# Head 0 built by engines, three hash passes instead of four, and a later landing time in the list schedule

## Chip, cores and metric

The kernel runs on one core of one Trainium2 chip. The metric is device time in microseconds (us) of one execution; the median of several runs is compared. Engines go by the profile's names: PE (matrix multiplication, with PEld for its weight loads), DVE (vector), ACT (activation), POOL (GpSimd) and SP, which here only issues DMA transfers.

## What is computed

Attention whose mask comes from a hash of q and k, followed by two dense blocks. The reference, cut to what matters:

```python
# q, k, v: (2, 8, 768, 64), proj: (64, 6); 16 heads in all
q_bits = (einsum('bhsd,dk->bhsk', q, proj) > 0); k_bits = the same of k
mask   = q_bucket[:, :, :, None] == k_bucket[:, :, None, :]     # all six bits equal
scores = where(mask, scale * q @ k.T, -1e9)
attn   = softmax(scores) @ v                                    # (+1e-9 below the sum)
x = attn as (1536, 512)
x = ((x @ w1) * (x @ w2)) @ w3 @ w_out                          # d_ff 1024
out = (sigmoid(x @ w_gate) * (x @ w_val)) @ w_out2              # d_ff 1536
```

The weights arrive as 64-bit floats and are decoded to 32 bits on the chip.

## The kernel before

**Stages.** The 16 heads are worked through one after the other, each in six score tiles g of 128 rows by 768 columns (96 in all). Beside them runs filler: the product of w3 and w_out (`gen_fill`), then the first dense block for the first 512 tokens (`gen_first`). After that `moe` does all the rest. Nearly all matrix products are split into a high and a low part of each operand and made of three passes.

**One head** (`prep`). q and k are transposed on PE and copied by ACT into `aq` and `ak`: rows 0 to 63 hold the high parts, rows 64 to 127 the low parts. A head's scores need four 128-row operands, `aq`, `bq`, `ak` and `bk`, put together by DMAs on SP's queue: `bq[0:64]` from `aq` (line 393), `bk[0:64]` from `ak`'s low rows (395), the hash rows `ft` into `bk[64:128]` and `bq[64:128]` (406, 407), and `ak[64:128]` from `ak`'s high rows (408). The hash rows come of a PSUM tile `gps` for each half of 384 columns: `aq` by the high and by the low part of the projection, then `ak` by both, four passes (401); DVE compares with zero (402). Head 0 has its own code, `first_head`: there the copies of `bq[0:64]` (433) and of `ak[64:128]` (436) are DMAs, and the rest is done by ACT and DVE. `prep` of the next head is spread over the current head's steps: the passes of `gps` come two steps after the transposes of q.

**One score tile.** Four matmuls (466, 469), a row maximum on DVE (476, 477), the exponential on ACT (487), transposes into two PSUM tiles `tp` (520), the split of those by ACT and DVE (523, 524), and for two tiles together twelve matmuls with v (537). `emit_x` brings the upper 64 rows of that result through ACT into a tile `xu` (546) and adds the lower ones on DVE (548).

**Shared things.** `tp`, `gps`, the transposes of q and k, the sums with v and the filler's accumulators (`w3t`, `wacc`, `p0`, `y0`) all come from one ring of four PSUM buffers, `psT` (line 285), which is handed out in program order. Weight tiles of 512 KB are loaded ahead by `stage_next` (318) and decoded by `decode` on ACT, POOL and DVE (334 to 343). Score tiles have two buffers, `scs`.

**Order.** Everything up to `moe` is put in order by a list schedule that runs while the kernel is built (`order_engines`): each engine takes the ready instruction with the lowest priority number, by costs written into the code. A transfer on SP's queue lands, by that model, 1080 ns after its issue plus bytes/360 ns plus 900 ns (lines 217 and 218). The resulting order is fixed for each engine; at run time an instruction that isn't ready holds up what is queued behind it on its engine. `Tiles.holds` adds one rule by hand: the fourth weight load may not be issued before the transfer named `late["c0"]`, which is line 433.

Of the kernel before, what the change touches and what calls it, by code (L numbers as in the profile page):

```python
# [44 lines left out]
def order_engines(tc):  # L45
# [122 lines left out]
    while events:  # L168
        now = events[0][0]
        while events and events[0][0] <= now:  # L170
            _, _, what, x = heapq.heappop(events)
            if what == "ready":
                heapq.heappush(ready[eng[x]], (ins[x].bass_priority, x))
            elif what == "slot":
                g = rings[x][0]
                slots[g] += 1
                pools[g[0]] -= 1
                wake(g)
                if not pools[g[0]]:
                    wake(g[0])  # L180
            elif what == "end":
                for u in ends[x]:
                    left[u] -= 1
                    at[u] = max(at[u], now + step.get((eng[x], eng[u]), 60))
                    if not left[u]:
                        post(at[u], "ready", u)
                for t in held.get(x, ()):
                    todo[t] -= 1
                    if not todo[t]:
                        post(now + 200, "slot", t)  # L190
        again = True
        while again:
            again = False
            for e in ranks:
                while free[e] <= now and ready[e]:
                    _, k = heapq.heappop(ready[e])
                    g = blocked(k)
                    if g is not None:
                        waiting.setdefault(g, []).append(k)
                        continue  # L200
                    for t in opens.get(k, ()):
                        g = rings[t][0]
                        slots[g] -= 1
                        taken[g] += 1
                        if slots[g] > 0 and waiting.get(g):
                            wake(g)
                            again = True
                    order[e].append(k)
                    for u in begins[k]:
                        left[u] -= 1  # L210
                        at[u] = max(at[u], now)
                        if not left[u]:
                            post(at[u], "ready", u)
                    free[e] = done = now + cost(k)
                    if e == "SP":
                        n = count(ins[k].outs[0]) * list(ins[k].outs[0].ap)[0][1] * mybir.dt.size(ins[k].outs[0].dtype)
                        dma = max(now + 1080, dma) + n / 360
                        done = dma + 900
                    post(done, "end", k)
                    post(free[e], "free", k)  # L220
    assert sum(map(len, order.values())) == N, "the list schedule is stuck"
# [7 lines left out]
def lsh_attention_moe_moe2_kernel(  # L229
# [48 lines left out]
    def f(ap):  # L278
        return ap.bitcast(F32)
# [8 lines left out]
    idr = cst.tile([P, P], F32R, name="idr")  # L288
    pq_raw = cst.tile([P, NB], F32, name="pq_raw")
    pq = [[cst.tile([P, P], F32R, name=f"pq{a}{i}") for i in range(2)] for a in "qk"]  # L290
    thr = cst.tile([P, 2], F32, name="thr")
    lim = cst.tile([P, 2], F32, name="lim")

# [16 lines left out]
    def stage_next():  # L310

        if units:
            dst, src = units.pop(0)
            alt[0] += 1
            other = late.get("mp") or (wp if "mw" not in late else dec)
            t = (other if alt[0] % 2 else dec).tile([P, CH], U64, tag="st", name="st", bufs=2)
            shp = dst.shape
            ld = sync.dma_start(out=t if len(shp) == 2 else t.rearrange("p (k f) -> p k f", k=shp[1]), in_=src)
            if "c0" in late and alt[0] == 4:
                Tiles.holds.append((ld.ins.name, late["c0"].name))  # L320
            staged.append((dst, t))

# [27 lines left out]
    def load_head(h, nms):  # L350
        if not 0 <= h < NH:
            return
        b, hh = divmod(h, H)
        for nm, src in (("q", q), ("k", k), ("v", v)):
            if nm in nms:
                t = ap_.tile([P, NT, D], F32, tag="raw" + nm, name=f"raw{nm}{h}", bufs=1)
                sync.dma_start(out=t, in_=src[b, hh].rearrange("(p c) d -> p c d", c=NT))
                raws[h, nm] = t

    def split(h, nm, part):  # L360
# [17 lines left out]
    def prep(h):  # L378

        load_head(h, "v")  # L380
        if h < NH:
            alloc_mats(h)
            m = mats[h]
            for nm, d in (("q", "aq"), ("k", "ak")):
                t = splits[h, nm]
                for half in range(2):
                    ps = psT.tile([P, 512], F32R, tag="t", name="trr")
                    for c in range(3):
                        pe.transpose(ps[:, c * P:(c + 1) * P], t[:, half * 3 + c].rearrange("p a d -> p (a d)"), idr)
                    act.activation(out=m[d][:, half * HS:(half + 1) * HS], in_=f(ps[:, :HS]), func=AF.Copy,  # L390
                                   scale=SCALE if nm == "q" else 1.0)
                    if nm == "q" and half == 1:
                        sync.dma_start(out=f(m["bq"][0:D]), in_=f(m["aq"][0:D]))
                    yield
            sync.dma_start(out=f(m["bk"][0:D]), in_=f(m["ak"][D:P]))
            for half in range(2):
                hs = slice(half * HS, (half + 1) * HS)
                ps = psT.tile([P, 512], F32, tag="t", name="gps")
                for n, nm in enumerate(("aq", "ak")):
                    for x in range(2):  # L400
                        pe.matmul(ps[:, :HS], lhsT=pq[n][x], rhs=m[nm][:, hs], start=n + x == 0, stop=n + x == 2)  # L401
                dve.tensor_scalar(out=m["ft"][:, hs], in0=ps[:, :HS], scalar1=thr[:, 0:1], scalar2=thr[:, 1:2],
                                  op0=ALU.is_gt, op1=ALU.mult)
                if half == 0:
                    yield
            sync.dma_start(out=f(m["bk"][D:P]), in_=f(m["ft"][0:D]))
            sync.dma_start(out=f(m["bq"][D:P]), in_=f(m["ft"][D:P]))
            sync.dma_start(out=f(m["ak"][D:P]), in_=f(m["ak"][0:D]))
            yield
        for nm in "qk":  # L410
            split(h + 1, nm, 0)
            split(h + 1, nm, 1)
        load_head(h + 2, "qk")
        split(h - 1, "v", 0)
        split(h - 1, "v", 1)

    def first_head():
# [6 lines left out]
        for nm, d in (("q", m["aq"]), ("k", kt)):  # L424
            t = splits[0, nm]
            for half in range(2):
                ps = psT.tile([P, 512], F32R, tag="t", name="trr")
                for c in range(3):
                    pe.transpose(ps[:, c * P:(c + 1) * P], t[:, half * 3 + c].rearrange("p a d -> p (a d)"), idr)
                kps = (kps + [ps])[-2:]  # L430
                act.activation(out=d[:, half * HS:(half + 1) * HS], in_=f(ps[:, :HS]), func=AF.Copy, scale=SCALE if nm == "q" else 1.0)
            if nm == "q":
                late["c0"] = sync.dma_start(out=f(m["bq"][0:D]), in_=f(m["aq"][0:D])).ins
        for half in range(2):
            act.activation(out=m["ak"][0:D, half * HS:(half + 1) * HS], in_=f(kps[half][0:D, :HS]), func=AF.Copy)
        sync.dma_start(out=f(m["ak"][D:P]), in_=f(kt[0:D]))
        for half in range(2):
            act.activation(out=m["bk"][0:D, half * HS:(half + 1) * HS], in_=f(kps[half][D:P, :HS]), func=AF.Copy)
        load_head(1, "qk")
# [100 lines left out]
    def emit_x(u):  # L540
        acc = av_t.pop(u)
        h, t = divmod(2 * u, NT)
        b, hh = divmod(h, H)
        r0 = (hh % 2) * D
        xu = ap_.tile([P, 2 * P], F32, tag="xu", name=f"xu{u}", bufs=1)
        act_copy(xu[r0:r0 + D], acc[D:P, :2 * P])
        x = xall[r0:r0 + D, hh // 2, b * S + t * P:b * S + (t + 2) * P]
        dve.tensor_tensor(out=x, in0=acc[0:D, :2 * P], in1=xu[r0:r0 + D], op=ALU.add)
        if t == NT - 2 and h % 2 == 1:
            emit_scale(h)  # L550

# [255 lines left out]
    for n, (r0, sg) in enumerate(((D, 1.0), (0, -1.0))):  # L807
        for x in range(2):
            dve.memset(f(pq[n][x]), 0.0)
        for b0, sgn in ((r0, sg), (r0 + o, -sg)):  # L810
            hi, lo = (t[:, b0:b0 + NB] for t in pq[n])
            dve.tensor_scalar(out=hi, in0=pq_raw, scalar1=sgn, scalar2=None, op0=ALU.mult)
            dve.scalar_tensor_tensor(out=lo, in0=pq_raw, scalar=sgn, in1=f(hi), op0=ALU.mult, op1=ALU.subtract)
    dve.memset(thr[D:P, 1:2], -BIG)
    dve.memset(thr[0:D, 1:2], 1.0)
    dve.memset(thr[:, 0:1], 0.0)
# [108 lines left out]
```

## Time and profile before

| | us |
|---|---|
| median of 3 runs | 849.06 (848.66 to 849.44) |
| profiled execution, its own time | 851.55 |
| span of that execution, first to last instruction | 849.0 |
| PE busy | 806.6 (95%) |
| DVE busy | 567.4 (67%) |
| ACT busy | 523.9 (62%) |
| mean granted clock of TensorE | 0.983 |

PE is busy for 95% of the span, but that is a mean over stages in which different engines are nearly full. The table of stretches shows each by itself. The granted clock is a share of full speed: 1.0 is 2.4 GHz, 0.5 is 1.2 GHz.

### The profile page before, as it was taken

How to read it: one execution, taken by the hardware profiler on the slowest of the kernel's cores; microseconds unless marked ns; L12 is line 12 of the kernel's file. 1: busy time of each engine (PE TensorE's matmuls, PEld its weight loads, DVE VectorE, ACT ScalarE, POOL GpSimd, SP SyncE). 2: the span in 40 equal slices, each digit the busy share in tenths (PEclk: the TensorE clock that was granted, in tenths of full speed). 3: DMA queues.
4: the chain of work that ended last, by engine and by line, in shares of the span. 5: the costliest groups of instructions: out<-in, count | busy, mean ns of one | idle time of the engine just before them, and what ended most of it. 6: DMA issues, size and time to landing. Idle time of an engine off the chain costs nothing.

```text
span 849.0 us, 12225 instructions
## 1 busy us (share of the span) xinstructions
PE 806.6 (95%) x4272; PEld 685.3 (81%) x4272; DVE 567.4 (67%) x967; ACT 523.9 (62%) x1024; POOL 336.6 (40%) x328
## 2 busy tenths in 40 slices
PE   4788999999989999999999989999999999999998
PEld 4677898989878989888788768778888888888886
DVE  5998988897889988997489999972222222222222
ACT  4887887877878998787356665653334333343331
POOL 2564334342345453338544546543332333323330
PEclk7898999999999999999999999999999999999999
DMA  7655554344335644221115443300001000010001
GB/s 225 176 177 169 160 133 130 88 108 109 85 106 134 159 126 104 83 91 54 50 49 160 153 134 122 127 0 1 1 0 38 14 1 0 1 50 1 0 1 49
DMA packets 44908, 71.54 MB, mean 84 GB/s; under 512 B 6128, under 2 KB 32752, under 8 KB 44848
## 3 DMA queue, kind: packets, MB, share of 16 engines
q1 hardware_dynamic: 44848, 70.78, 29.2%
q8 instruction: 33, 0.54, 0.3%
q14 instruction: 27, 0.22, 0.1%
HBM read 52.43 MB, written 3.19 MB: 66 GB/s over the span
## 4 chain that ended last, share of the span: by engine, by line
PE 69%; DVE 18%; issue 6%; ACT 4%; DMA 3%; SPq 0%; DVEq 0%; ACTq 0%
PE pa L698 12%; PE pb L698 12%; PE m L698 11%; PE av L537 6%; PE tp L520 6%; PE p L698 5%; PE wacc L593 4%; PE s L466 3%; DVE da L337 3%; PE s L469 3%; DVE da L338 3%; PE gps L401 2%; PE y L698 2%; DVE pt L524 2%; DVE s L476 1%
## 5 line engine op out<-in xcount | busy, mean ns | idle before, releaser
L738 DVE TENSOR_TENSOR pb<-pb,a 128x512 f32<-128x512 f32 x52 | 36.2, 695 | 138.8 <-PE pb L698 134.8
L336 POOL TENSOR_SCALAR da<-da 128x512 f32<-128x512 f32 x76 | 54.1, 712 | 137.3 <-ACT da L334 136.3
L524 DVE TENSOR_TENSOR pt<-tp,pt 128x384 fp32r<-128x384 f32 x192 | 101.1, 549 | 6.5 <-ACT pt L523 4.9
L520 PE MATMUL tp<-idf,e 128*128 128x128 f32 x576 | 101.2, 278 | 3.1 <-ACT ak L390 1.4
L487 ACT ACTIVATE e<-s,sm 128x768 f32<-128x768 f32 x96 | 95.8, 999 | 13.0 <-DVE sm L477 12.8
L692 POOL TENSOR_TENSOR wal<-xall,wah 128x512 fp32r<-128x512 f32 x36 | 46.9, 1302 | 137.9 <-ACT wah L276 137.9
L523 ACT ACTIVATE pt<-tp 128x384 fp32r<-128x384 f32 x192 | 90.3, 494 | 17.9 <-PE tp L520 16.1
L476 DVE TENSOR_REDUCE s<-s 128x1 f32<-128x768 f32 x96 | 91.9, 957 | 13.0 <-PE s L469 12.8
L698 PE MATMUL pa<-x,wah 128*128 128x512 f32 x320 | 98.9, 389 | 0.0
L698 PE MATMUL pb<-x,wbh 128*128 128x512 f32 x320 | 98.5, 389 | 0.0
L520 PEld LDWEIGHTS tp<-idf,e 128*128 128x128 f32 x576 | 72.7, 143 | 14.7 <-ACT ak L390 2.3
L537 PE MATMUL av<-pt,spv 128*128 128x256 f32 x576 | 79.5, 289 | 0.2 <-DVE pt L524 0.2
L334 ACT ACTIVATE da<-st 128x512 f32<-128x512 f32 x76 | 51.0, 671 | 43.9 <-DVE w1r L343 17.9
L537 PEld LDWEIGHTS av<-pt,spv 128*128 128x128 f32 x576 | 73.5, 194 | 2.6 <-DVE pt L524 0.6
L466 PE MATMUL s<-ak,aq 128*128 128x384 f32 x192 | 63.7, 389 | 10.4 <-ACT e L487 8.9
L593 PE MATMUL wacc<-wo,t 128*128 128x512 f32 x192 | 70.5, 427 | 0.5 <-ACT wo L276 0.2
L698 PEld LDWEIGHTS pb<-x,wbh 128*128 128x128 f32 x320 | 60.1, 188 | 12.4
L698 PEld LDWEIGHTS pa<-x,wah 128*128 128x128 f32 x320 | 60.1, 188 | 12.4
L338 DVE SCALAR_TENSOR_TENSOR da<-st,da 128x512 uint32<-128x512 uint32 x76 | 65.9, 867 | 1.3
L698 PE MATMUL pb<-x,wbl 128*128 128x512 f32 x160 | 62.2, 389 | 0.0
L698 PE MATMUL pa<-x,wal 128*128 128x512 f32 x160 | 62.2, 389 | 0.0
L469 PE MATMUL s<-bk,bq 128*128 128x384 f32 x192 | 59.0, 367 | 0.0
(159 smaller groups left out, 1899.1 us busy)
## 6 DMA issues: line engine op xcount, KB each, us to landing
st<-in_moe_w_dram SPq DMA_DIRECT2D x32, 512.0 KB, 3.9
st<-in_moe_w_out_dram SPq DMA_DIRECT2D x20, 512.0 KB, 3.5
st<-in_moe_w_gate_dram SPq DMA_DIRECT2D x12, 512.0 KB, 3.5
st<-in_moe_w_val_dram SPq DMA_DIRECT2D x12, 512.0 KB, 3.6
rawq<-in_q_dram SPq DMA_DIRECT2D x16, 192.0 KB, 3.1
rawk<-in_k_dram SPq DMA_DIRECT2D x16, 192.0 KB, 3.7
rawv<-in_v_dram SPq DMA_DIRECT2D x16, 192.0 KB, 2.4
bq<-aq SPq DMA_DIRECT2D x16, 192.0 KB, 2.6
```

The costliest lines, as they stand in the source:

```text
L336: pool.tensor_scalar(out=f(a), in0=f(a), scalar1=F64_HI, scalar2=F64_LO, op0=ALU.min, op1=ALU.max)
L338: dve.scalar_tensor_tensor(out=a, in0=hw, scalar=0xC0000000, in1=a, op0=ALU.bitwise_and, op1=ALU.bitwise_or)
L466: pe.matmul(s[:, half, :HS], lhsT=m["aq"][:, qs], rhs=m["ak"][:, ks], start=True, stop=False)
L469: pe.matmul(s[:, half, :HS], lhsT=m["bq"][:, qs], rhs=m["bk"][:, ks], start=False, stop=True)
L476: dve.tensor_reduce(out=one[:, 1:2], in_=s[:, :, :HS], op=ALU.max, axis=AX.XY, negate=True)
L487: act.activation(out=e.rearrange("p (a c) -> p a c", a=2), in_=s[:, :, :HS], func=AF.Exp, bias=sm[:, 1:2], scale=sm[:, 0:1], accum_out=su_ ...
L520: pe.transpose(ps[:, j * P:(j + 1) * P], e[:, c * P:(c + 1) * P], idf)
L523: act.activation(out=dh, in_=src, func=AF.Copy)
L524: dve.tensor_tensor(out=lo[:, g % 2, half * 3:half * 3 + 3], in0=src, in1=f(dh), op=ALU.subtract)
L537: pe.matmul(acc[:, :2 * P].rearrange("p (a t) -> p a t", a=2), lhsT=w, rhs=r[:, :, c], start=(c == 0 and i == 0), stop=(c == NT - 1 and i ...
L593: pe.matmul(acc, lhsT=t3[x][:, j], rhs=wo[y][:, j], start=(j == 0 and n == 0), stop=(j == NF1 - 1 and n == 2))
L698: mm = pe.matmul(ps, lhsT=lhs[x], rhs=rhs[y], start=start and n == 0, stop=stop and n == 2)
```

## The change

Five edits:

- Head 0: `bq[0:64]` is copied by POOL instead of a DMA. `ak[64:128]` is copied by DVE straight from the PSUM tiles of the transposed k, instead of a DMA from SBUF.
- Head 0's loads: the third weight load, not the fourth, is held, until head 1's load of k is issued.
- Heads 1 to 15: the hash rows take three passes instead of four. The third pass multiplies `bq`, whose lower rows hold the high rows of q and whose upper rows get a copy of the high rows of k by one more DMA, with a new constant `pl` that holds both low parts of the projection. The product of the low part of the projection with the low parts of q and k is no longer formed. The upper rows of `bq` are overwritten with hash rows later, as before.
- `emit_x`: ACT writes the upper rows straight into `xall`, and DVE adds in place; the tile `xu` is gone.
- The list schedule takes a transfer to land 2400 ns instead of 900 ns after its last byte.

```diff
-                        done = dma + 900
+                        done = dma + 2400
...
+    pl = cst.tile([P, P], F32R, name="pl")
...
-            if "c0" in late and alt[0] == 4:
+            if "c0" in late and alt[0] == 3:
...
-                sync.dma_start(out=t, in_=src[b, hh].rearrange("(p c) d -> p c d", c=NT))
+                ld = sync.dma_start(out=t, in_=src[b, hh].rearrange("(p c) d -> p c d", c=NT))
+                if h == 1:
+                    late["c0"] = ld.ins
...
+            sync.dma_start(out=f(m["bq"][D:P]), in_=f(m["ak"][0:D]))
             sync.dma_start(out=f(m["bk"][0:D]), in_=f(m["ak"][D:P]))
...
-                for n, nm in enumerate(("aq", "ak")):
-                    for x in range(2):
-                        pe.matmul(ps[:, :HS], lhsT=pq[n][x], rhs=m[nm][:, hs], start=n + x == 0, stop=n + x == 2)
+                for n, nm in enumerate(("aq", "ak", "bq")):
+                    pe.matmul(ps[:, :HS], lhsT=pq[n][0] if n < 2 else pl, rhs=m[nm][:, hs], start=n == 0, stop=n == 2)
...
-                late["c0"] = sync.dma_start(out=f(m["bq"][0:D]), in_=f(m["aq"][0:D])).ins
+                pool.tensor_copy(m["bq"][0:D], f(m["aq"][0:D]))
...
-            act.activation(out=m["ak"][0:D, half * HS:(half + 1) * HS], in_=f(kps[half][0:D, :HS]), func=AF.Copy)
-        sync.dma_start(out=f(m["ak"][D:P]), in_=f(kt[0:D]))
+            hs = slice(half * HS, (half + 1) * HS)
+            act.activation(out=m["ak"][0:D, hs], in_=f(kps[half][0:D, :HS]), func=AF.Copy)
+            dve.tensor_copy(m["ak"][D:P, hs], f(kps[half][0:D, :HS]))
...
-        xu = ap_.tile([P, 2 * P], F32, tag="xu", name=f"xu{u}", bufs=1)
-        act_copy(xu[r0:r0 + D], acc[D:P, :2 * P])
         x = xall[r0:r0 + D, hh // 2, b * S + t * P:b * S + (t + 2) * P]
-        dve.tensor_tensor(out=x, in0=acc[0:D, :2 * P], in1=xu[r0:r0 + D], op=ALU.add)
+        act_copy(x, acc[D:P, :2 * P])
+        dve.tensor_tensor(out=x, in0=acc[0:D, :2 * P], in1=x, op=ALU.add)
...
+    for n in range(2):
+        (act_copy if n else dve.tensor_copy)(pl[n * D:(n + 1) * D], f(pq[n][1][n * D:(n + 1) * D]))
```

## Rows read from the trace of the kernel before

**Rows 1.** Busy time by stretch, all engines; clock 1.00 is full speed.

```profile
core 0: us, PE busy (x) PEld busy (x) DVE busy (x) ACT busy (x) POOL busy (x), PEclk, DMA share, GB/s
0.00:20.00 20.00, 8.26 (x36) 7.50 (x36) 11.23 (x40) 9.08 (x17) 3.81 (x11) 0.80 0.81 237
20.00:83.00 63.00, 52.32 (x305) 44.26 (x304) 59.01 (x109) 52.34 (x107) 32.87 (x36) 0.88 0.59 170
83.00:100.00 17.00, 15.92 (x108) 14.17 (x106) 16.14 (x30) 13.20 (x28) 8.87 (x10) 0.99 0.50 141
100.00:220.00 120.00, 118.06 (x798) 106.47 (x797) 104.21 (x202) 94.30 (x200) 36.78 (x46) 1.00 0.45 117
220.00:240.00 20.00, 15.58 (x112) 14.00 (x111) 16.93 (x34) 17.12 (x37) 11.63 (x12) 1.00 0.46 117
240.00:383.00 143.00, 140.39 (x936) 126.70 (x935) 129.48 (x256) 121.79 (x259) 61.14 (x67) 0.99 0.42 112
383.00:435.00 52.00, 51.50 (x229) 42.18 (x228) 33.79 (x37) 28.58 (x52) 33.41 (x23) 1.00 0.13 41
435.00:565.00 130.00, 124.22 (x531) 98.22 (x530) 123.81 (x160) 82.84 (x149) 65.38 (x61) 1.00 0.39 122
565.00:849.00 284.00, 280.30 (x1237) 231.85 (x1235) 72.81 (x105) 104.69 (x177) 82.72 (x64) 1.00 0.03 12
```

**Rows 2.** Timeline 0 to 20: start, duration, engine, line, instruction, idle before it.

```profile
5.94 1.00 POOL L369 TENSOR_TENSOR spv<-rawv,spv 128x384 fp32r<-128x384 f32 x1 [4.64 <-DVE spv L366]
8.05 0.62 SPq L436 DMA_DIRECT2D ak<-ft  x1
8.56 1.25 DVE L450 TENSOR_SCALAR bk<-gps,thr 64x384 fp32r<-64x384 f32 x2 [2.70 <-PE gps L447]
9.83 1.29 DVE L450 TENSOR_SCALAR bq<-gps,thr 64x384 fp32r<-64x384 f32 x2
13.08 0.62 DVE L366 CAST spq<-rawq 128x384 fp32r<-128x384 f32 x1 [1.96 <-DMA rawq<-in_q_dram]
16.25 0.36 DVE L366 CAST spk<-rawk 128x384 fp32r<-128x384 f32 x1 [0.80 <-DMA rawk<-in_k_dram]
17.11 1.01 PE L466 MATMUL s<-ak,aq 128*128 128x384 f32 x2 [1.48 <-DMA ak<-ft]
17.91 0.84 PE L469 MATMUL s<-bk,bq 128*128 128x384 f32 x2
18.80 0.97 DVE L476 TENSOR_REDUCE s<-s 128x1 f32<-128x768 f32 x1 [1.12 <-PE s L469]
```

**Rows 3.** Chain that ended last, in order of time: start, duration, what.

```profile
8.05 9.02 DMA ak<-ft
254.45 1.39 PE gps L401 x8
```

**Rows 4.** Timeline around head 15's hash rows, 338 to 345.

```profile
338.19 0.82 PE L520 MATMUL tp<-idf,e 128*128 128x128 f32 x6
338.19 0.46 SPq L395 DMA_DIRECT2D bk<-ak  x1
339.55 0.51 PE L401 MATMUL gps<-aq,pqq 128*128 128x384 f32 x2
340.44 0.68 DVE L402 TENSOR_SCALAR ft<-gps,thr 128x384 fp32r<-128x384 f32 x1
341.42 0.51 PE L401 MATMUL gps<-aq,pqq 128*128 128x384 f32 x2
342.83 0.67 DVE L402 TENSOR_SCALAR ft<-gps,thr 128x384 fp32r<-128x384 f32 x1
```

**Rows 5.** DMA issues by tile: count, KB each, median us from issue to landing.

```profile
bk<-ak SPq DMA_DIRECT2D x15, 192.0 KB, 2.7
bq<-ft SPq DMA_DIRECT2D x15, 192.0 KB, 4.1
```

**Rows 6.** Timeline, head 11: its last transfer issued, its first score matmuls.

```profile
257.43 0.61 SPq L407 DMA_DIRECT2D bq<-ft  x1
268.01 0.52 PE L466 MATMUL s<-ak,aq 128*128 128x384 f32 x2
```

**Rows 7.** What PE waited for, 0 to 385: us, times, longest.

```profile
PE s L466 <- ACT e L487: 8.9, 7, 4.1
PE trr L389 <- DVE pt L524: 2.6, 5, 1.0
PE tp L520 <- DVE xall L548: 1.2, 3, 0.6
```

**Rows 8.** Groups of instructions, whole span: busy us, mean ns, idle before.

```profile
L366 POOL CAST spk<-rawk 128x384 fp32r<-128x384 f32 x14 | 7.9, 568 | 15.1 <-PE trr L389 14.8 <-DMA rawk<-in_k_dram 0.3
L276 ACT ACTIVATE xu<-av 64x256 f32<-64x256 f32 x48 | 18.3, 380 | 15.5 <-PE av L537 14.3
L548 DVE TENSOR_TENSOR xall<-av,xu 64x256 f32<-64x256 f32 x48 | 19.9, 415 | 13.5 <-ACT xu L276 12.8
```

**Rows 9.** Busy time in a stretch of half clock, columns as in rows 1.

```profile
76.00:84.00 8.00, 6.83 (x29) 6.33 (x30) 5.81 (x12) 4.59 (x9) 1.21 (x3) 0.57 0.49 177
```

## Prediction

> **What bounds the kernel now.** I read the busy time by stretch first, because the mean of 95% PE hides which engine is full where. In [rows 1] the first 20 us are bound by nothing that is busy: PE works 8.26 us of them, DVE 11.23. From 20 to 83 DVE works 59.01 of 63 us (94%) and PE 83%, so DVE sets the pace there. From 83 to 383 PE works 290.0 of 300 us (15.92, 118.06, 15.58 and 140.39) and DVE 88%: PE is the bound, and the only gap worth the name is the 4.4 us in 220 to 240. After 383 the change touches no instruction; PE is the bound from 383 to 435 and from 565 to the end, DVE from 435 to 565. A shift of the first 383 us should therefore be passed on whole.
>
> Then I read the timeline of the first 20 us [rows 2]. The hash rows of head 0 are done at 9.83 + 1.29 = 11.12, but the first scores start at 17.11, and the row names what they wait for: the DMA that copies `ak`. The chain [rows 3] gives its price, 9.02 us from issue to landing. Its own row and the DMA column of [rows 1] say why: at 0.81 share and 237 GB/s it stands behind the first weight loads.
>
> **Head 0.** With POOL and DVE copies, what comes last for the first score tile is the first half of the hash rows of q: `bq` is written by two instructions from 9.83 on, the first done near 10.5. `ak`'s DVE copies lie in the gap of 2.70 us before 8.56 [rows 2]. They aren't in the trace; the nearest rows are the two compares of 64x384 out of PSUM, 1.25 us, and half of that would be a gain on nothing, so I take 1.25 and it fits the gap. POOL's copy of 768 columns is at most twice a cast of 384 columns, 2 x 0.568 = 1.14 us [rows 8]; put before POOL's 1.00 us at 5.94 it ends near 7.1, behind it near 8.1, in both cases before 10.5. So the covers hold by over 1 us; gone, they would cost the same amount at most.
>
> The first row maximum can then start at about 10.5 + 0.2 + 0.84 (the second pair of score matmuls at the pace of [rows 2]) = 11.6 to 11.8, in place of 18.80: 7.0 us sooner. Not all of that is a gain, since DVE is what is full from 20 us on. The gain is DVE's idle time that gets filled. In [rows 2] the gaps are 1.96 (wait for the load of head 1's q), 0.80 (load of its k) and 1.12 (first scores). The last two vanish: there is softmax work to do, and the new hold lets the load of k pass a weight load of 512 KB, some 2 us at 237 GB/s. Of 1.96 I take away 1.0, as the first maximum (0.97) fits into it. 1.0 + 0.80 + 1.12 = **2.9 us**. Bounds: 0, if DVE's decode work was going to fill later gaps anyway, and 7.0, if everything moves with the first scores.
>
> The Trainium skill, on the page "SBUF — State Buffer", section "Who interferes with whom", holds that a POOL instruction and a DVE copy or cast in its two-port mode block each other for a whole instruction. By that rule the cast at 4.08 to 5.86 could lose up to one POOL copy, and the first scores would come up to 1.1 us later, a time near 845.6, inside the range of the forecast. No row here shows that pair; the copies read PSUM.
>
> **Three passes.** Eight passes of a head take 1.39 us in a run without a break [rows 3], 0.174 each. Two of eight fall away: 0.35 us a head. Heads 4 to 15 have them in the stretch that PE bounds, 12 x 0.35 = **4.2 us**. Heads 1 to 3 have them while DVE is full, so I count nothing there (5.2 if they count).
>
> **The price of the third pass.** It needs a copy of `ak`'s high rows in `bq`, by a DMA that can't be issued before `ak` is complete. In [rows 4] the sister copy is issued at 338.19, just as `ak` is done; the first pass runs at 339.55, 1.4 us later, and the compare ends at 341.12. A copy of this kind lands 2.7 us after issue [rows 5], and the new list schedule allows it 1080 + 546 + 2400 ns = 4.0 us, so it will put the third pass at about 342.2 and the compare near 343.3: each half keeps its PSUM buffer up to 2.2 us longer than the 1.6 us of today (the second half is less, 0.6 here). Both halves together take two of the four `psT` buffers, a filler accumulator mostly the third, so the transposes have one for a while. What is queued behind on PE isn't stuck, as the schedule knows of the wait and fills it with scores, sums with v and filler, as far as buffers allow. PE waits little [rows 7] for readers of that ring today (2.6 and 1.2 us). The buffers lost are 3 to 6 buffer-us a head, that is 0.7 to 1.5 us if all four were always in demand. Lower end nothing, upper end 1.0 us a head or 12 us. I take 0.2 us a head, **2.5 us** over 12 heads, nearer to the low end since DVE and ACT have a tenth of their time free there [rows 1] and can catch up.
>
> The DMAs behind it (lines 406 to 408) go out later by 1 to 3 us. They are due when the next head's scores begin: head 11 has the last one issued at 257.43 and its first scores at 268.01 [rows 6], and 4.1 us of landing [rows 5] leave 6.5 us. So that costs nothing; with the cover gone, at most what exceeds it. The added DMA waits on SP for what its neighbour, line 395, waits for already, so nothing new is stuck behind it; its issue is 0.46 us [rows 4].
>
> **In place, and the order.** ACT's 380 ns and DVE's 415 ns stay as they are, and ACT waited for PE there, not for the single buffer of `xu` [rows 8]: nothing. The constant `pl` costs two small copies at 5 us, in idle time. The later landing time shifts every consumer of a transfer in the order. At run time hardly any engine waits for a transfer after 20 us; it can mend little, and can move decode work behind where it was wanted, above all in the gap of 220 to 240. PE's idle time between 83 and 383 is 10.0 us [rows 1]; a new order may win or lose some 4 of it, about the size of that gap. I take 0.
>
> **Sum.** The profiled execution's span is 849.0 us, its own time 851.55; the median of the runs is 849.06, 2.49 below that, and I subtract from the median. 849.06 - 2.9 - 4.2 + 2.5 = **844.5 us**.
>
> **Rivals.**
> - *The ring is full* (slower). The third pass waits with two of four buffers held, and transposes starve behind it. At 1.0 us a head it is 849.06 - 7.1 + 12 = 854.0. It decides the sign from 7.1/12 = 0.6 us a head on. For it: the ring has four buffers for everything. Against: [rows 7].
> - *The clock falls in the new waits* (slower). Each time PE idled, at the start, its clock was at half afterwards, and from 76 to 84 it was 0.57 in the mean with PE 6.83 us busy [rows 9]; at full clock that work is 6.83 x 0.57 = 3.9 us, so such a spell costs up to 2.9 us where PE is the bound. Three new ones give 844.5 + 8.8 = 853.3. The Trainium skill tells this on "TensorE: Matmul & The Clock Gate", section "HAM oscillation": waits for a DMA in each turn of a loop leave PE cold for the next. The trace shows it only where PE had little to do, not in 100 to 220.
> - *It does little* (same). Head 0's gain is swallowed by DVE, which is full to 83 either way, and the third pass's wait eats most of the passes: 849.06 - 1 - 4.2 + 4 = 847.9 and above.
> - *More of it arrives* (faster). The first scores' full 7.0 us arrive, all fifteen heads' passes count, and nothing is lost: 849.06 - 7.0 - 5.2 = 836.9.
>
> **How the numbers follow.** A measurement tells about 0.2%, 1.7 us, from no change. My forecast, with times of 841 to 847.3, has 0.46; the larger gain 0.17; little (847.3 to 850.8) 0.14; the full ring 0.18 and the clock 0.05. Faster 0.63, same 0.14, slower 0.23. With a tenth cut off on either side the range goes from 838.5, near the large gain, to 853.5, between the two slow cases. The forecast's own range is 841 to 847.3.
>
> **What the profile would show.** Right: first scores near 10 to 12 us and DVE with no gap of over 1 us between 12 and 20; 90 passes in `gps` instead of 120; a busy share of PE in 100 to 383 as now, with the end of the attention stage 4 to 5 us sooner. Wrong: waits of PE for readers of `psT` of more than 10 us in sum, or of the third pass for the copy; new stretches of half clock; a gap in 220 to 240 that has grown. If the first scores are 7 us sooner and 83 us comes no sooner, the DVE step is wrong; if the passes are gone and PE's idle time takes their place, the price of the third pass is.

## The result

The changed kernel takes 855.02 us in the median of 4 runs, against 849.25 us of the kernel before on the same chip: a ratio of 1.0065, 95% interval 1.0049 to 1.0081. It is slower by 5.8 us where I forecast 4.6 us less; the measured time lies above the top of the range.

The same stretches as in [rows 1], of the changed kernel (columns as there):

```profile
0.00:20.00 20.00, 11.57 (x54) 10.23 (x55) 14.37 (x47) 11.79 (x23) 5.04 (x13) 0.83 0.66 217
20.00:83.00 63.00, 49.59 (x305) 39.72 (x304) 62.36 (x110) 52.08 (x109) 33.23 (x38) 0.97 0.65 178
83.00:100.00 17.00, 14.72 (x95) 12.57 (x94) 16.88 (x30) 12.10 (x25) 6.64 (x8) 1.00 0.64 187
100.00:220.00 120.00, 117.25 (x786) 103.51 (x785) 102.66 (x200) 94.00 (x201) 37.28 (x48) 1.00 0.46 121
220.00:240.00 20.00, 16.55 (x116) 14.25 (x115) 17.86 (x36) 17.38 (x39) 10.08 (x10) 1.00 0.48 126
240.00:383.00 143.00, 139.07 (x913) 121.98 (x913) 128.94 (x249) 118.46 (x255) 58.81 (x66) 1.00 0.40 111
383.00:435.00 52.00, 49.06 (x203) 39.78 (x202) 36.09 (x41) 28.12 (x51) 30.66 (x22) 0.93 0.20 61
435.00:565.00 130.00, 125.48 (x540) 99.96 (x538) 122.43 (x156) 82.57 (x149) 65.88 (x61) 1.00 0.38 122
```

In the first 20 us DVE does 14.37 us of work in place of 11.23 and PE 11.57 in place of 8.26: the head start is there. Between 83 and 383 the same work should have taken PE 24 matmuls less; it is busy 287.6 us and not 290.0, and has got through 1910 matmuls and not 1954 (the counts of the four rows added up). So the PE-bound stretch is worse, and in 383 to 435 PE has 2.9 us of idle time, where [rows 1] has 0.5.

The last sum with v is added at 383.23 (the row is shown below), and in the kernel before at:

```profile
383.70 0.42 DVE L548 TENSOR_TENSOR xall<-av,xu 64x256 f32<-64x256 f32 x1 [1.35 <-ACT xu L276]
```

Of the lead of 7.3 us that the first maximum had, 0.5 is left there, and all of the 4.6 us between the two spans (849.0 and 853.6) lies behind the attention stage. One execution against another is coarse, though. In f2 below, the kernel before with one unread copy added, PE, DVE, ACT and POOL work in exactly the order of the kernel before, and this addition starts at 379.92, 3.8 us sooner; between 20 us and there TensorE has half the clock for 13.7 us in f2 and for 19.1 in the kernel before.

The start, from the timeline, against [rows 2]:

```profile
5.70 0.92 POOL L436 CAST bq<-aq 64x768 fp32r<-64x768 f32 x1 [4.40 <-ACT aq L434]
7.53 1.02 DVE L440 CAST ak<-trr 64x384 fp32r<-64x384 f32 x2 [1.58 <-ACT ak L439]
10.02 1.29 DVE L454 TENSOR_SCALAR bq<-gps,thr 64x384 fp32r<-64x384 f32 x2
10.85 0.95 PE L473 MATMUL s<-bk,bq 128*128 128x384 f32 x4 [0.80 <-DVE bq L454]
11.47 0.97 DVE L480 TENSOR_REDUCE s<-s 128x1 f32<-128x768 f32 x1 [0.17 <-PE s L473]
```

The first row maximum starts at 11.47 (11.6 to 11.8 was worked out), and what comes last before it is the hash half of `bq`, as said. The two copies took 1.02 and 0.92 us (1.25 and at most 1.14 in the prediction).

Head 15's hash rows, against [rows 4] (line 398 is the new copy, 404 the passes, 405 the compare):

```profile
335.67 0.47 SPq L398 DMA_DIRECT2D bq<-ak  x1
337.23 0.40 PE L404 MATMUL gps<-aq,pqq 128*128 128x384 f32 x1
337.47 0.34 PE L404 MATMUL gps<-ak,pqk 128*128 128x384 f32 x1
338.36 0.34 PE L404 MATMUL gps<-aq,pqq 128*128 128x384 f32 x1
338.54 0.34 PE L404 MATMUL gps<-ak,pqk 128*128 128x384 f32 x1
340.10 0.51 PE L404 MATMUL gps<-bq,pl 128*128 128x384 f32 x2
340.48 1.26 DVE L405 TENSOR_SCALAR ft<-gps,thr 128x384 fp32r<-128x384 f32 x2
```

The third pass runs 4.4 us after the copy is issued. The first half's buffer is open from 337.23 to about 341.1 and the second's from 338.36 to 341.74, 3.9 and 3.4 us, in place of 1.6 and 2.1 in [rows 4]. Over heads 4 to 15 the mean from the first pass to the end of the compare is 4.69 us for the first half, before 1.85, and 4.19 for the second, before 1.80.

What PE waited for in 0 to 400, against [rows 7] (only readers of `psT`; five of its rows):

```profile
PE tp L524 <- DVE pt L528: 3.9, 5, 1.3
PE gps L404 <- DVE pt L528: 2.8, 4, 1.4
PE trr L392 <- DVE pt L528: 1.8, 1, 1.8
PE tp L524 <- DVE ft L405: 1.8, 4, 0.5
PE tp L524 <- DVE xall L551: 1.1, 4, 0.6
```

They sum to 11.4 us. The prediction named over 10 us of such waits as the sign that its price of the third pass is wrong. In the kernel before, rows of these kinds sum to 5.2 us: the 2.6 and 1.2 of [rows 7] and

```profile
PE gps L401 <- DVE pt L524: 0.8, 1, 0.8
PE tp L520 <- DVE pt L524: 0.4, 1, 0.4
PE gps L401 <- DVE ft L402: 0.2, 1, 0.2
```

### The profile page after: what moved, and what is told of

Its sections match the earlier page's. It is cut to its first block, busy times and chain, and to the rows that moved or that the text cites. A ratio compares the mean times of both kernels' runs of the same rounds, so it can differ in the third digit from the quotient of the medians.

```text
span 853.6 us, 12206 instructions
## 1 busy us (share of the span) xinstructions
PE 806.3 (94%) x4242; PEld 675.6 (79%) x4242; DVE 577.9 (68%) x970; ACT 523.0 (61%) x1025; POOL 333.3 (39%) x329
## 4 chain that ended last, share of the span: by engine, by line
PE 60%; DVE 24%; issue 7%; ACT 5%; DMA 2%; POOL 1%; SPq 0%; DVEq 0%; ACTq 0%; POOLq 0%
PE pa L701 12%; PE pb L701 12%; PE m L701 11%; PE av L541 5%; PE wacc L596 4%; DVE da L339 4%; PE tp L524 4%; DVE da L338 4%; PE p L701 3%; DVE pt L528 3%; PE s L470 3%; DVE s L480 2%; PE s L473 2%; PE trr L392 1%; DVE wtl L695 1%
## 5 line engine op out<-in xcount | busy, mean ns | idle before, releaser
L701 PE MATMUL pa<-x,wah 128*128 128x512 f32 x320 | 101.7, 397 | 2.9 <-DVE x L684 1.6
L480 DVE TENSOR_REDUCE s<-s 128x1 f32<-128x768 f32 x96 | 92.0, 958 | 18.3 <-PE s L473 17.5
L524 PEld LDWEIGHTS tp<-idf,e 128*128 128x128 f32 x576 | 70.4, 141 | 25.4 <-DVE pt L528 6.9
L541 PE MATMUL av<-pt,spv 128*128 128x256 f32 x576 | 77.2, 283 | 5.0 <-DVE pt L528 3.7
L541 PEld LDWEIGHTS av<-pt,spv 128*128 128x128 f32 x576 | 70.9, 188 | 9.8 <-DVE ft L405 3.0
L335 ACT ACTIVATE da<-st 128x512 f32<-128x512 f32 x76 | 51.3, 675 | 42.8 <-DVE w1r L344 20.0
L339 DVE SCALAR_TENSOR_TENSOR da<-st,da 128x512 uint32<-128x512 uint32 x76 | 72.9, 960 | 1.5
```

The costliest lines, as they stand in the source:

```text
L339: dve.scalar_tensor_tensor(out=a, in0=hw, scalar=0xC0000000, in1=a, op0=ALU.bitwise_and, op1=ALU.bitwise_or)
L480: dve.tensor_reduce(out=one[:, 1:2], in_=s[:, :, :HS], op=ALU.max, axis=AX.XY, negate=True)
L524: pe.transpose(ps[:, j * P:(j + 1) * P], e[:, c * P:(c + 1) * P], idf)
L541: pe.matmul(acc[:, :2 * P].rearrange("p (a t) -> p a t", a=2), lhsT=w, rhs=r[:, :, c], start=(c == 0 and i == 0), stop=(c == NT - 1 and i ...
L701: mm = pe.matmul(ps, lhsT=lhs[x], rhs=rhs[y], start=start and n == 0, stop=stop and n == 2)
```

## The experiments

The parts were first done alone, then the third pass was taken apart. Ratios are against runs of the kernel before on the same chip.

| run | what | median us | before there | ratio, 95% interval |
|---|---|---|---|---|
| e1_landing | landing 2400 ns alone | 842.65 | 850.29 | 0.9907 (0.9887 to 0.9927) |
| e2_head0 | head 0 alone | 846.08 | 850.29 | 0.9950 (0.9930 to 0.9969) |
| e3_passes | three passes alone | 858.24 | 850.29 | 1.0096 (1.0063 to 1.0130) |
| e4_all_land900 | whole change, landing 900 | 852.80 | 850.29 | 1.0037 (1.0021 to 1.0052) |
| f1_nowait | e3 without the wait (leaves a product out) | 845.88 | 850.05 | 0.9952 (0.9931 to 0.9973) |
| f2_copyonly | the copy alone | 850.06 | 850.05 | 1.0009 (0.9991 to 1.0027) |
| f3_poolcopy | e3, copy by POOL | 848.08 | 850.05 | 0.9979 (0.9966 to 0.9992) |
| e6_all_four | whole change, four passes | 843.43 | 850.05 | 0.9916 (0.9885 to 0.9947) |
| g1_copy900 | whole, the copy at 900 ns | 849.16 | 849.75 | 1.0001 (0.9986 to 1.0016) |
| f4_all_poolcopy | whole, copy by POOL | 844.40 | 849.75 | 0.9948 (0.9931 to 0.9964) |
| h1_land1650 | landing 1650 alone | 846.97 | 849.75 | 0.9968 (0.9955 to 0.9982) |
| h2_land3300 | landing 3300 alone | 842.60 | 849.75 | 0.9925 (0.9910 to 0.9939) |
| k1_all_later | whole, passes a step later | 844.14 | 849.32 | 0.9929 (0.9907 to 0.9950) |
| k2_passes_later | e3, a step later | 849.19 | 849.32 | 0.9996 (0.9981 to 1.0011) |
| k3_before_later | before, a step later | 846.16 | 849.32 | 0.9964 (0.9950 to 0.9978) |
| k4_pool_later | whole, POOL and later | 845.43 | 849.68 | 0.9954 (0.9940 to 0.9968) |
| k5_four_later | e6, a step later | 847.20 | 849.68 | 0.9974 (0.9963 to 0.9984) |
| k6_all_nowait | whole without the wait (leaves a product out) | 838.29 | 849.68 | 0.9869 (0.9851 to 0.9887) |

Differences below are taken between ratios, times 849.25 us, as the chips differ by up to 1 us. Where a difference is split by stage, it is one execution against one, and coarse by some 4 us.

### The parts alone

The theory after the result was "ring": the third pass holds two of four PSUM buffers while it waits. The rival was "order": the later landing draws a worse fixed order.

e1 is the first hunk of the diff, by itself. 

> The kernel before with the later landing (2400 ns) in the list schedule alone. Theory 'order': the later landing puts instructions into a worse fixed order and is the loss; then about 853 to 856 us. Theory 'ring': the loss is the third pass that waits for its copy with PSUM buffers held; then this stays within 1 us of 849.2.

e2 is the hunks of `first_head`, `load_head` and the hold. 

> The kernel before with the head 0 edits alone (POOL and DVE copies, third weight load held). The orders of all engines are those of before except in the first part. Both theories: 2 to 4 us faster, 845 to 847, since the trace of the changed kernel is about 3 us ahead through most of the attention stage. If it stays at 849, the lead is not worth anything at the end.

e3 is the hunks with `pl`, the copy and the loop of the passes. 

> The kernel before with three hash passes alone, landing 900 ns in the schedule. Theory 'ring': slower, 851 to 855, with PE waits for readers of the PSUM ring or for the copy. Theory 'order': faster by the 4 us of passes less a little hold, 845 to 848.

e4 is everything with

```diff
-                        done = dma + 2400
+                        done = dma + 900
```

> The whole change but with the landing left at 900 ns. Theory 'order': 843 to 847. Theory 'ring': as slow as the whole change, 853 to 856, or worse, since the schedule then expects the copy sooner than it lands.

"Order" fell at once: the later landing alone is worth -7.9 us, which neither theory had, and the whole change without it (e4) is slower than before as well. Head 0 alone is worth -4.2 us, within the 845 to 847 us of its expectation. Three passes alone cost +8.2 us, more than the whole change and more than "ring" had said. In e3 PE has 5.9 us of direct waits for the copy between 83 and 383:

```profile
PE gps L402 <- DMA bq<-ak: 5.9, 3, 3.2
```

### The third pass taken apart

f1 keeps everything of e3, the copy too, and takes the reader away from it. It leaves out the product of the low part of the projection with k:

```diff
-                    pe.matmul(..., rhs=m[nm][:, hs], start=n == 0, stop=n == 2)
+                    pe.matmul(..., rhs=m[nm if n < 2 else "aq"][:, hs], start=n == 0, stop=n == 2)
```

> Three passes alone on the kernel before (landing 900 ns), but the third pass reads aq, which is there long since, in place of the copy in bq; the copy is still issued. This leaves the low part of the projection without its product with k, so the computed hash differs in the last digits. Same number of passes, no wait for the copy. Theory 'ring' (the wait for the copy, with PSUM buffers held, is the loss): 844 to 847, that is 849 to 850 less the 4 us of passes. Theory 'fewer passes do not pay in PE's stretch' or 'the DMA is the loss': 850 or more.

f2 is the kernel before with the one line of the copy added. 

> The kernel before with the one added DMA a head (the high rows of k into bq) and nothing that reads it; PE, DVE, ACT and POOL keep the order of before. Theory 'ring': no change, 849 to 851. Theory 'the DMA on SP's queue is the loss' (it delays what is issued behind it): 853 to 858.

f3 replaces the DMA of e3:

```diff
-            sync.dma_start(out=f(m["bq"][D:P]), in_=f(m["ak"][0:D]))
+            for half in range(2):
+                hs = slice(half * HS, (half + 1) * HS)
+                pool.tensor_copy(m["bq"][D:P, hs], f(m["ak"][0:D, hs]))
```

> Three passes alone, the copy into bq made by POOL in two halves instead of a DMA, so that it is there about 1.5 us after ak is done and not 4. Theory 'ring': most of the loss goes, 845 to 850. If the loss is that the order is another one, whatever the wait: 853 to 858 as with the DMA.

The copy costs nothing that can be measured (f2, with PE, DVE, ACT and POOL in the order of before). Three passes without a wait are worth -4.1 us (f1), the 4.2 us of the prediction. With the wait they cost +8.2: the wait is worth 12.2 us. Up to 5.9 of these may be PE standing at the copy itself, by the row above; in the changed kernel, whose schedule puts the third pass later, no such row is left. Halfway, with a copy that is there sooner, they are worth -1.8 (f3). One view shows the difference, PE's row for 83 to 383 in e3 and, below it, in f1:

```profile
83.00:383.00 300.00, 285.51 (x1891) 251.79 (x1890) 264.99 (x508) 242.43 (x517) 116.79 (x132) 0.99 0.45 120
```

```profile
83.00:383.00 300.00, 291.52 (x1941) 261.67 (x1940) 267.49 (x520) 249.78 (x531) 121.56 (x136) 0.99 0.48 127
```

In the same 300 us e3 gets through 50 matmuls less, and DVE and ACT through 12 and 14 instructions less: all three are held back together. The last sum of the attention stage is added at 388.90 in e3 and at 376.63 in f1, 12.3 us apart; the two spans, 853.5 and 844.2, are 9.3 apart, so the loss lies inside the stage and 2.9 us of it come back behind.

### The whole change without its third pass, and without its wait

e6 takes the three-pass hunks out of the whole change. 

> The whole change with four hash passes as before: head 0 by engines, in-place sum, landing 2400 ns. If head 0 (4 us) and the later landing (7 us) add up: 838 to 840. If both are the same gain at the start of the kernel: 842 to 845.

k6 is the edit of f1 in the whole change. 

> The whole change, but the third pass reads aq in place of the copy in bq, so that it waits for nothing; the copy is still issued. This leaves the low part of the projection without its product with k. It gives the price of the wait in the whole change: theory 'held buffers': 838 to 842, below the same change with four passes (843.4) by up to the 4 us of passes. If the passes are not on the bound here: about 843.

Head 0 and the later landing don't add up: together with the in-place sum they are worth -7.1 us (e6), no more than the landing alone (-7.9). Without the wait the whole change is worth -11.1 us, 838.29 us (k6), and 4.0 of that against e6 are the passes. So in the whole change the wait costs 1.0065 - 0.9869, or 16.6 us. k6's row from 83 to 383:

```profile
83.00:383.00 300.00, 291.63 (x1939) 261.94 (x1938) 265.06 (x516) 247.23 (x526) 119.64 (x135) 0.99 0.46 125
```

By the traces, 7.0 of the 16.4 us between the spans are made inside the attention stage. These rows end it: the last addition of a sum with v, in the changed kernel and in k6.

```profile
383.23 0.42 DVE L551 TENSOR_TENSOR xall<-av,xall 64x256 f32<-64x256 f32 x1
```

```profile
376.27 0.42 DVE L551 TENSOR_TENSOR xall<-av,xall 64x256 f32<-64x256 f32 x1
```

The first accumulator of `moe`'s second product opens at 433.98 and 420.54, which is 13.4 us apart: the handover from the attention stage to `moe` gives another 6.5. These are the rows of the handover, from the end of that addition to that accumulator, in the changed kernel and in k6:

```profile
383.64:433.98 50.34, 47.40 (x195) 38.40 (x194) 34.46 (x38) 27.40 (x50) 30.10 (x22) 0.93 0.20 63
```

```profile
376.69:420.54 43.85, 43.85 (x195) 36.25 (x194) 32.52 (x37) 26.74 (x49) 30.51 (x21) 1.00 0.18 60
```

PE has the same 195 matmuls in both. In the changed kernel it is idle for 2.9 us, in its first two matmuls of `pa`, which wait for ACT (1.3 us) and DVE (1.6 us):

```profile
PE pa L701 <- DVE x L684: 1.6, 1, 1.6
PE pa L701 <- ACT wah L276: 1.3, 1, 1.3
```

During the second of these waits its granted clock falls to the lower level, 1.2 GHz. Half of PE's 6.20 us in the row below, 3.1, is most of the 3.6 us by which its 195 matmuls are longer:

```profile
391.60:398.40 6.80, 6.20 (x15) 4.85 (x16) 6.80 (x6) 5.89 (x12) 6.80 (x5) 0.50 0.50 167
```

The last 3.0 us come in `moe` behind that, where DVE is busy 199.81 us in the changed kernel and 197.15 in k6. That this second half is the wait's doing is not shown. k6 and the changed kernel don't share their orders after the start, and over all kept traces the handover takes 43.9 to 51.3 us: the longest is that of f1, which has no wait, with a spell of half clock of its own, and e3, with the wait, has 48.4.

### Why the later landing gains alone and loses with the third pass

e4 and the whole change differ in the landing alone, and here it costs 2.4 us. g1 gives the schedule 900 ns for the one new copy and 2400 for the rest. 

> The whole change, but the schedule takes the one new copy (high rows of k into bq) to land after 900 ns and every other transfer after 2400. It tells why the later landing gains alone and loses with the three passes. Theory 'it lengthens the hold' (the schedule puts the third pass 1.5 us later, buffers are held longer): faster than the whole change by 3 to 6 us, 849 to 852. Theory 'the orders just differ': anywhere from 848 to 857, with no link to the hold.

h1 and h2 are e1 with other values. 

> The kernel before with a landing of 1650 ns. Its orders are those of before again after about the first fifth of the work. If the gain of the later landing is made at the start: most of it is here, 843 to 846. If it is made in the rest of the order: 848 to 850.

> The kernel before with a landing of 3300 ns. If the gain comes of landing times near those on the chip, 3300 ns is past them and gives part of it back, 843 to 848. If each value just draws another order: anywhere from 840 to 856.

g1 is 5.4 us faster than the whole change, as "it lengthens the hold" has it. By the traces the mean time from first pass to first compare is 3.88 us in g1, 3.97 in e4 and 4.69 in the whole change. So the later landing makes the schedule hold the buffers 0.7 to 0.8 us longer.

The loss follows the hold. Against the runs without a wait, both halves together hold their buffers 4.1 us longer a head in e3, 4.1 in g1 and 5.8 in the changed kernel (means of heads 4 to 15). A quarter of that, as the ring has four buffers, is 12.3, 12.2 and 17.5 us over 12 heads; the losses are 12.2, 11.2 and 16.6. The fit is of three cases, and by the traces part of the last loss lies behind the attention stage. Runs whose hold is nearly cured (f3, and f4, k1, k2 and k4 below) have 0.6 to 0.8 us of it left, 1.9 to 2.5 us by that rule, and lose 2.3 to 7.2: at that size the scatter of the orders hides it.

Alone, the landing gains 2.7 us with 1650 ns, 7.9 with 2400 and 6.4 with 3300. The last is no third value: PE, DVE, ACT and POOL work through h2 in the order of e1 from the first instruction to the last, and only some DMA issues change places. So 7.9 and 6.4 are nearly one kernel measured on two chips, and what other values draw was not tried. For 1650 the orders are those of before again after about a fifth of the work, so its gain, which lies between its two expectations, must come of the order at the start; how isn't shown. DVE is busy 61.41 us of 63 in 20 to 83 there and 61.14 in e1, where [rows 1] has 59.01, but f2, in the order of before, has 61.81:

```profile
20.00:83.00 63.00, 52.24 (x319) 43.52 (x317) 61.81 (x113) 54.86 (x114) 35.83 (x37) 0.95 0.69 189
```

By the traces e1's gain lies behind the attention stage, which ends at 380.36 in e1 and at 380.34 in f2, while the spans are 841.0 and 847.2. DVE does more of its work early there, 42.10 us in 383 to 435 in e1 and 37.10 in f2; first e1's rows, then f2's:

```profile
383.00:435.00 52.00, 52.00 (x231) 43.05 (x230) 42.10 (x49) 32.22 (x59) 35.34 (x26) 1.00 0.15 47
435.00:565.00 130.00, 126.58 (x546) 101.19 (x545) 117.41 (x151) 80.35 (x144) 66.68 (x60) 1.00 0.36 114
```

```profile
383.00:435.00 52.00, 51.55 (x227) 42.18 (x226) 37.10 (x42) 28.18 (x52) 31.74 (x23) 1.00 0.09 27
```

### Held buffers or late hash rows

The passes can be given out one step of the attention loop later, so that the copy has landed when they open. The hash rows are then as late as in the changed kernel, or later, but no buffer is held:

```diff
-    PAT = (2, 2, 2, 0, 0, 0)
+    PAT = (2, 2, 0, 2, 0, 0)
```

k1 does it to the whole change. 

> The whole change with the hash passes given out one step of the attention loop later (PAT 2,2,0,2,0,0), so that the copy by DMA has landed when their PSUM tiles open. Theory 'held buffers': the loss of the third pass goes, 840 to 845, though the hash rows come as late as before or later. Theory 'late hash rows': no better than the whole change, 853 to 858.

k2 does it to e3. 

> Three passes by DMA alone on the kernel before (landing 900 ns), given out one step later. Theory 'held buffers': near the run without a wait, 845 to 849. Theory 'late hash rows': 855 to 860, as with three passes alone.

k3 does it to the kernel before. 

> The kernel before, four passes, given out one step later: the control for what the later place costs by itself. Theory 'held buffers': 848 to 852. Theory 'late hash rows': slower by several us, 853 or more.

k1 is 11.5 us faster than the whole change, k2 8.5 faster than e3 (0.2 us above its expected 849), and late hash rows cost the kernel before nothing (k3 gains 3.1). The copy is issued at 333.46 and the first pass of head 15 runs at 337.67 in k1; all three passes of a half follow each other:

```profile
333.46 0.47 SPq L398 DMA_DIRECT2D bq<-ak  x1
337.67 0.33 PE L404 MATMUL gps<-aq,pqq 128*128 128x384 f32 x1
337.85 0.34 PE L404 MATMUL gps<-ak,pqk 128*128 128x384 f32 x1
338.02 0.34 PE L404 MATMUL gps<-bq,pl 128*128 128x384 f32 x1
338.74 0.68 DVE L405 TENSOR_SCALAR ft<-gps,thr 128x384 fp32r<-128x384 f32 x1
```

The buffer is open for 1.75 us; the mean over heads 4 to 15 is 1.95, in the changed kernel 4.69. "Late hash rows" has fallen.

### Other remedies, and how far orders scatter

f4 is the whole change with the copy by POOL, as in f3. 

> The whole change with the copy made by POOL in two halves instead of the DMA. Theory 'ring': the loss of the third pass goes and the gains of head 0, of the later landing and of the passes remain, 838 to 843. If the passes still lose: 846 or more.

k4 has POOL's copy and the later step. 

> The whole change with the copy by POOL and the passes given out one step later, both remedies at once: if what is left in each of them (844.1 and 844.4) is a remainder of the hold, 839 to 842; if it is the order, 843 to 846.

k5 is e6 with the later step. 

> Head 0, in-place sum and later landing with four passes, given out one step later: 840 to 842 if the later place is worth its 3 us here too, 843 to 845 if not. Against the same with three passes and the copy by DMA (844.1) it tells whether three passes pay at all.

POOL's copy takes 9.9 us of loss away (f4), more than half of what k6 says is there, but ends 1.4 above its expected 843. k4 has both remedies and is no better than either. k5 says why such remainders shouldn't be read: the same move of one step gains 3.1 us in the kernel before and loses 4.9 in e6, outside both ranges of its expectation. With four passes and with three the whole change takes 847.2 and 844.1 at the later step; at the earlier one, with POOL's copy, it is 843.4 and 844.4. Whether three passes pay against four, once the wait is cured in a way that computes the hash, is open: the scatter between two orders, some 4 us either way, is as large as the passes.

Of what computes everything, e1 (ratio 0.9907) and e6 (0.9916) are the fastest, their intervals overlap, and h2, which is e1's order again, and k1 are just behind. Both e1 and e6 keep the four passes of before.

## Why the prediction was wrong

**What bounds it, head 0, the passes.** Right in the main. A shift of the first part was passed on: head 0 alone is -4.2 us for my 2.9, and the passes without a wait -4.1 for my 4.2. The first maximum was 7.3 us sooner than in [rows 2], and DVE had no gap over 1 us between 12 and 20. Wrong was that behind 383 all stays as it is because no instruction is touched there: an edit of what stands before can change the order of the handover too, and its length differs by up to 7.4 us between the runs.

**The price of the third pass.** This is the step that failed. The mechanism was named. The hold was sized nearly right for the first half, where 2.2 us longer was worked out and 2.84 was the mean, and too short for the second, 0.6 against 2.39; the sum, 5.2 buffer-us a head, is within my 3 to 6. The price wasn't right. I took 0.2 us a head, 2.5 in all, and 12 as the far end; measured are 12.2 (e3 against f1) and 16.6 us (the whole change against k6), past that end. The case that I had worked out and set aside, all four buffers always in demand, 0.7 to 1.5 us a head, is the one that fits: 1.0 and 1.4.

I leaned to the low end because PE seldom waited for the ring and DVE and ACT had a tenth of their time free there. The waits were read too low, as [rows 7] has 3.8 of the 5.2 us. And few waits for a buffer tell that four buffers were enough for the order then drawn, not that they were too many: with the longer hold the waits in `psT`'s rows came to 11.4 us, and DVE's spare time didn't give it back, as PE, ACT and DVE were held back together (e3 and f1). I counted the loss inside the attention stage alone. By the traces that is where it is made in e3 (12.3 us, with 2.9 given back behind); of the changed kernel's 16.4 us between the spans 7.0 lie there and 9.4 behind.

**The later landing.** I took 0 with 4 either way. Alone it is -7.9 us. It was right that hardly any engine waits for a transfer after 20 us; wrong that it can therefore mend little. It moved DVE's work to where DVE had room, which [rows 1] could have told: in 383 to 435 DVE was busy 33.79 of 52 us, just ahead of a stretch in which it is the bound. How the whole 7.9 us come of that isn't shown. Within the change, the same edit lengthened the hold (g1).

**In place.** Nothing was forecast, and it wasn't run by itself.

**The rivals.** The one that came true is "the ring is full", at 0.18; it gave 854.0 us and the time is 855.0. Its size is a coincidence: it has 12 us of hold where 16.6 were measured, and no gain for the landing. "The clock falls in the new waits" did not come true: from 83 to 383 the granted clock is 1.00 in every row of the changed kernel. The 0.93 in 383 to 435 is the one new dip; it came with a wait of PE, as the rival had it, and cost some 3 us, but f1 has such a dip without the third pass's wait, and the mean granted clock of the execution is 0.989, in k6 0.986. "More of it arrives" gave 836.9, and k6, a kernel without the wait, takes 838.3. That is near in the number alone: head 0 and all fifteen heads' passes were to bring it, where e6 and k6 have 7.1 us of head 0 and landing together and 4.0 of the passes.

**Cover.** That the transfers of the hash rows and of `ak[64:128]` (406 to 408 before, 409 to 411 now) have slack held: k3 shows that hash rows a step later cost nothing.

**What stays open.** That the loss is the wait with open buffers is shown by shortening the hold in four ways (no wait, POOL's copy, a shorter landing for the copy, a later step). That it acts through the four buffers of the ring is argued from the waits and the fit, as the number of PSUM buffers was never changed. How much of the 9.4 us behind the attention stage is a must, and how much the order that happened to be drawn, can't be told from runs whose orders scatter by 4 us.

## What to carry to other kernels

An accumulation that starts before its last operand is there turns a transfer's latency into buffer time; price it by how long how many buffers of the shared ring are held, and where the ring is small take the high end, as if every buffer were always in demand, however few waits the trace shows. Start such a group only when all its operands are there, or drop the pass that needs the late one. In a kernel whose order is drawn by a list schedule, change one thing at a time and look also at what the order does at the next stage's start: a parameter of the model was worth more here than head 0 or the passes.

## What the runs showed of the hardware beyond that

DVE's instructions lengthen beside POOL's. One step of the decode, which works on two SBUF inputs, took 960 ns in the mean in the changed kernel and 867 before; over 76 of them that is 7 us more DVE time for the same work:

```profile
L339 DVE SCALAR_TENSOR_TENSOR da<-st,da 128x512 uint32<-128x512 uint32 x76 | 72.9, 960 | 1.5
```

```profile
L338 DVE SCALAR_TENSOR_TENSOR da<-st,da 128x512 uint32<-128x512 uint32 x76 | 65.9, 867 | 1.3
```

In the changed kernel the 20 of them that no POOL instruction overlaps took 672 to 693 ns, and the other 56 took 674 to 2246. In the kernel before, the step's neighbour, which has one SBUF input, takes 0.42 us at 25.07, where POOL starts 0.17 us behind it, and 1.52 at 34.95, where POOL has started 0.04 us ahead and works to 36.19:

```profile
25.07 0.42 DVE L337 TENSOR_SCALAR da<-da 128x512 uint32<-128x512 uint32 x1
25.24 0.72 POOL L336 TENSOR_SCALAR da<-da 128x512 f32<-128x512 f32 x1 [1.58 <-ACT da L334]
34.91 1.28 POOL L588 TENSOR_TENSOR wo<-wor,wo 128x512 fp32r<-128x512 f32 x1 [2.26 <-ACT wo L276]
34.95 1.52 DVE L337 TENSOR_SCALAR da<-da 128x512 uint32<-128x512 uint32 x1
```

The Trainium skill, "SBUF — State Buffer", section "Who interferes with whom", says that a DVE instruction in a two-port mode, which `tensor_scalar` can enter, and a POOL instruction exclude each other for a whole instruction, and that a DVE instruction with two SBUF inputs contends with a POOL instruction that reads SBUF. The trace agrees: the second DVE instruction ends 0.28 us after POOL's, and the first, which came before POOL's, isn't lengthened. So in a stretch that DVE bounds, which POOL instruction the order puts beside which DVE instruction is part of DVE's time, and it is one way in which two orders of the same work differ. It isn't what made the loss here. Up to the end of the attention stage DVE is busy as long in k1 as in the changed kernel (the rows below, in this order), and k1 ends the stage 5.9 us sooner:

```profile
0.00:377.73 377.73, 349.53 (x2256) 304.60 (x2257) 344.25 (x670) 308.82 (x649) 155.45 (x181) 0.98 0.50 140
```

```profile
0.00:383.64 383.64, 349.40 (x2261) 302.79 (x2262) 343.67 (x667) 306.24 (x648) 151.09 (x180) 0.99 0.49 135
```
